# Turning x and the softmax's weights in 32-wide blocks on VectorE instead of on TensorE, from the fourth batch on

## The chip, the cores and the metric

One Trainium2 chip, one core, one launch. The metric is the device time of the whole kernel in microseconds, the median of three runs. Beside it stands one profiled execution, whose trace is what the rows below are read from.

## What is computed

```
q, k, v: (8 batches, 8 heads, 576 positions, 64)           float32
mask: heads 0-3 local (0 <= row - col < 32); heads 4-7 strided (row >= col, row % 32 == col % 32)
attn = softmax(q @ k.T / 8 where mask) @ v
x = attn, heads side by side: (8, 576, 512)
xn = (x - mean) / sqrt(var + 1e-6) * g_ln                  # over the last axis
out = x + relu(xn @ w_ch1) @ w_ch2                         # 512 -> 2048 -> 512
```

## The kernel before, in words

**Two parts in one stream.** The attention of a batch makes x; the feed-forward (FFN) part takes x in chunks of 512 positions, one per batch (positions 0 to 511), and a ninth chunk of the last 64 positions of all batches. Products are exact enough because each operand is held as a high and a low float32r part, and three products are summed (high-high, high-low, low-high).

**Steps.** A run is one chunk; run c does chunk c, in 16 steps f = 0 to 15, one per 128 hidden columns (`steps`, L1005). In a step TensorE does `ffn1` (L758: 12 matmuls into the PSUM tile `ph`, of which there is one), then two halves of `ffn2` (L771: 12 matmuls) with the hidden activations of the step before. From `ph` ScalarE makes `hh` (L749) and VectorE `hl` (L754); `ph` is free for the next `ffn1` when `hl` is made. The runs go in the order 1, 0 (its second half), 2, 3, ... 8; LayerNorm's scale is applied at the end, from x loaded back from DRAM (`residual`, L794, at f = 9 to 14; `close`, L815, in the first step of the next run).

**Visits.** The attention of batches 2 to 7 is woven into the steps. A Pair is two heads of one batch; pairs alternate local and strided, four to a batch, 32 in all. Generator `visits` (L991) makes one visit for each pair i from 7 on, and the main loop takes one piece of it in each step for which `slots[n]` (L1009) is true, between `ffn1` and the first half of `ffn2`. Before, from run 2 on these are the even f, and a visit has two pieces:

- first piece (f = 0, 4, 8, 12): `scores_and_values` (L592). TensorE multiplies the turned weights of pair i (`pt`) by its v, and q by k for pair i+1 (tile `sv`, L637). For pair i+1 VectorE adds the mask (L459) and takes the maximum (L471), GpSimd subtracts it (L475), ScalarE takes the exponential (L480) into `sm`. For pair i VectorE scales the values into `xo` (L649) and SyncE's queue stores `xo` into DRAM (`x_store`, L530; `xdl` for local pairs, `xds` for strided ones, rows in another order). Then v of pair i+2 is loaded (`load_v`, L391), on SyncE's queue.
- second piece, two steps later: `weights_and_x` (L656). TensorE transposes x of pair i (4 tiles of 128x128 for a local pair, 6 for a strided one) and the weights of pair i+1 (6 or 5 tiles) into PSUM (tile `px`, L668). ScalarE makes the high part of x from `px` (L577), VectorE the low part (L582), ScalarE copies the turned weights out (`pt`, L673), and VectorE sums the softmax's rows (L677 to L679, tile `den`).

In the step after a first piece `turn` (L984) turns q and k of pair i+2 on VectorE (`t_half`, L412: L416 local, L418 strided; instruction STREAM_TRANSPOSE, which turns each 32x32 block by itself) from tile `raw`, and then issues the loads of q and k of pair i+3 into the one `raw` buffer (`load_qk`, L328: eight DMAs on SyncE's queue, each 32 partitions by 18 pieces of 32 values, 128 bytes apiece). The loads put the blocks where 32x32 turns make a whole turn of them.

Each engine and each DMA queue takes its instructions in the order of the program (L1098 to L1107). A DMA that waits holds back what stands behind it in its queue. All buffers of the visits (`raw`, `xo`, `pt`, `px`/`sv`) are single.

Of the kernel before, what the change touches and what calls it, by code (L numbers as in the profile page):

```python
# [8 lines left out]
F32 = mybir.dt.float32  # L9
# [37 lines left out]
def kernel(  # L47
# [10 lines left out]
    nc = tc.nc  # L58
# [132 lines left out]

    w1b, w2b = w1.bitcast(U32), w2.bitcast(U32)
# [121 lines left out]
    class Pair:  # L314
# [13 lines left out]
        def load_qk(self):  # L328

            self.raw = raw_tile(f"raw{self.id}").rearrange("p (i s) -> p i s", i=2)  # L330
            for i, src in enumerate((q, k)):
                for h in range(2):
                    for d in range(2):
                        p0 = 64 * h + 32 * d
                        nc.sync.dma_start(  # L335
                            self.raw[p0:p0 + 32, i].rearrange("p (g e) -> p g e", e=32),
                            src[self.b, self.h0 + h].rearrange("(g t) d -> t g d", t=32)[
                                :, :, 32 * d:32 * d + 32])
# [52 lines left out]
        def load_v(self, once=False):  # L391
            dma = nc.sync.dma_start
# [159 lines left out]

        def x_views(self):
# [102 lines left out]
    def weights_and_x(px, p):  # L656
# [14 lines left out]
        if p:  # L671
            p.pt = smp.tile([P, NS, P], F32, tag="pt", name=f"pt{p.id}")
            nc.scalar.copy(out=p.pt[:, 0:p.nt].rearrange("p t x -> p (t x)"),  # L673
                           in_=ps[:, P * n_x:P * (n_x + p.nt)])
            den = stp.tile([P, 2, NS], F32, tag="den", name=f"den{p.id}", bufs=2)
            p.den = den[:, :, 0:p.nt]
            nc.vector.reduce_sum(p.den, p.smv, axis=AX.X)  # L677
            nc.vector.tensor_scalar(p.den, p.den, 1e-9, None, op0=ALU.add)
            nc.vector.reciprocal(out=p.den, in_=p.den)  # L679
# [304 lines left out]
    def turn():  # L984
        while todo:
            i = todo.pop()
            pairs[i].t_piece()
            if 2 * NHP <= i + 1 < NP:
                pairs[i + 1].load_qk()

    def visits():  # L991

        for i in range(2 * NHP - 1, NP):
            p = pairs[i + 1] if i + 1 < NP else None
            pv = pairs[i] if i >= 2 * NHP else None
            scores_and_values(pv, p)
            turned(i + 2)
            if pv and i + 2 < NP:
                pairs[i + 2].load_v()
            yield  # L1000
            weights_and_x(pv, p)
# [6 lines left out]
    for n, (r, f) in enumerate(steps):  # L1008
        slots[n] = (r is runs[1] and f in (11, 13) or r is runs[2]  # L1009
                    or r is not runs[1] and r.c + 1 < B and f % 2 == 0)  # L1010
# [127 lines left out]
```

## Time and profile before

| | |
|---|---|
| median of 3 runs | 928.85 us (927.37 to 929.29) |
| the profiled execution, its own time | 928.84 us |
| span of the profiled execution | 927.1 us |
| TensorE matmul busy | 908.8 us, 98% of the span |
| TensorE weight load busy | 748.5 us, 81% |
| VectorE, ScalarE, GpSimd busy | 409.6, 225.0, 155.4 us (44%, 24%, 17%) |
| granted TensorE clock, mean over the span | 0.995 of full speed |

The span is what the trace covers; 1.7 us of the execution's time lie around it. Matmuls are pipelined, so the busy time of TensorE counts overlaps; what a group of matmuls takes from the whole is read from the chain of work that ended last, where each piece starts at the end of the piece before it.

### The profile page before, as it was taken

What the parts mean: (1) busy time and instruction counts of PE and PEld (TensorE: products, weight loads), DVE (VectorE), ACT (ScalarE), POOL (GpSimd) and SP (SyncE); (2) the same over time, 40 slices, a digit from 0 to 9 for tenths busy, and PEclk for the clock granted to TensorE, in tenths of its full rate; (3) what the DMA queues carried; (4) which work ended last, traced back from release to release, by engine and by line L of the source; (5) the groups of instructions that cost most, each with busy time, mean ns of one, the idle gap of its engine ahead of it and who ended that gap; (6) DMA issues with size and microseconds to landing.
All of it is one profiled execution on the core that took longest, in us unless ns stands there. A gap on an engine that the chain in (4) does not pass through costs nothing.

```text
span 927.1 us, 18224 instructions
## 1 busy us (share of the span) xinstructions
PE 908.8 (98%) x7668; PEld 748.5 (81%) x7668; DVE 409.6 (44%) x784; ACT 225.0 (24%) x378; POOL 155.4 (17%) x191
## 2 busy tenths in 40 slices
PE   6899999999999999999999999999999999999997
PEld 4678888888888888888888888888888888888886
DVE  5887573447743354435433453434443321122123
ACT  4765563112212111211112121112121111111110
POOL 6776385101100010001000110001000000000000
PEclk9999999999999999999999999999999999999999
DMA  9989961247652435243423334243511130002001
GB/s 202 213 181 262 235 201 35 38 100 158 117 105 52 98 64 109 53 76 86 104 40 59 85 64 89 48 98 64 109 28 48 36 108 18 0 1 91 1 1 45
DMA packets 227353, 81.62 MB, mean 88 GB/s; under 512 B 180560, under 2 KB 218184, under 8 KB 227272
## 3 DMA queue, kind: packets, MB, share of 16 engines
q1 hardware_dynamic: 226344, 79.93, 38.4%
q8 instruction: 60, 0.98, 0.4%
q10 hardware_dynamic: 928, 0.53, 0.2%
q14 instruction: 21, 0.17, 0.1%
HBM read 60.25 MB, written 20.18 MB: 87 GB/s over the span
## 4 chain that ended last, share of the span: by engine, by line
PE 93%; DMA 3%; SPq 2%; ACT 0%; DVE 0%; issue 0%; POOL 0%; DVEq 0%; POOLq 0%
PE po L768 42%; PE ph L739 28%; PE ph L743 14%; PE sv L637 5%; PE px L668 3%; DMA rows<-in_k_dram 2%; PE po_last L768 1%; DMA s<-in_moe_w_ch_dram 1%; SPq L335 1%; DMA v_l<-in_v_dram 1%; SPq L346 0%; SPq L406 0%; PE cm L262 0%; SPq L350 0%; PE px L727 0%
## 5 line engine op out<-in xcount | busy, mean ns | idle before, releaser
L768 PE MATMUL po<-w,hh 128*128 128x512 f32 x1120 | 351.3, 395 | 0.8 <-DVE hl L754 0.8
L754 DVE SCALAR_TENSOR_TENSOR hl<-ph,hh 128x512 fp32r<-128x512 f32 x144 | 99.6, 692 | 448.4 <-ACT hh L749 448.4
L768 PEld LDWEIGHTS po<-w,hh 128*128 128x128 f32 x1120 | 205.4, 188 | 42.6 <-ACT pt L490 0.9
L739 PE MATMUL ph<-xh,w 128*128 128x512 f32 x568 | 222.2, 391 | 0.0
L739 PE MATMUL ph<-xl,w 128*128 128x512 f32 x568 | 221.1, 389 | 0.0
L768 PE MATMUL po<-w,hl 128*128 128x512 f32 x560 | 218.1, 390 | 0.0
L749 ACT ACTIVATE hh<-ph 128x512 fp32r<-128x512 f32 x144 | 86.0, 597 | 501.5 <-PE ph L743 501.2
L743 PE MATMUL ph<-xh,w 128*128 128x512 f32 x568 | 152.2, 390 | 0.0
L743 PEld LDWEIGHTS ph<-xh,w 128*128 128x128 f32 x568 | 106.6, 188 | 22.3
L739 PEld LDWEIGHTS ph<-xh,w 128*128 128x128 f32 x568 | 106.7, 188 | 21.9
L739 PEld LDWEIGHTS ph<-xl,w 128*128 128x128 f32 x568 | 106.7, 188 | 21.8
L768 PEld LDWEIGHTS po<-w,hl 128*128 128x128 f32 x560 | 105.1, 188 | 22.4
L475 POOL TENSOR_TENSOR sm<-sm,mx 128x640 f32<-128x640 f32 (+1 forms) x32 | 40.6, 1270 | 358.9 <-DVE mx L471 358.9
L720 POOL TENSOR_TENSOR rs<-rs,mhalf 128x1 f32<-128x1 f32 x36 | 19.7, 549 | 354.5 <-DVE rs L719 354.5
L480 ACT ACTIVATE sm<-sm 128x640 f32<-128x640 f32 (+1 forms) x32 | 23.7, 742 | 106.0 <-POOL sm L475 106.0
L582 DVE TENSOR_TENSOR xl<-px,xh 128x512 fp32r<-128x512 f32 (+2 forms) x48 | 29.9, 661 | 14.4 <-ACT xh L577 14.3
L577 ACT ACTIVATE xh<-px 128x512 fp32r<-128x512 f32 (+2 forms) x48 | 27.5, 646 | 14.7 <-PE px L668 11.2
L231 DVE SCALAR_TENSOR_TENSOR p<-s,p 128x512 uint32<-128x512 uint32 x32 | 22.1, 690 | 11.9 <-ACT p L227 11.8
L471 DVE TENSOR_REDUCE mx<-sm 128x10 f32<-128x640 f32 (+1 forms) x32 | 26.3, 822 | 1.8
L827 DVE SCALAR_TENSOR_TENSOR x<-po,rs,x 128x512 f32<-128x512 f32 (+1 forms) x36 | 24.4, 729 | 1.4 <-PE po L768 1.1
L673 ACT COPY pt<-px 128x640 f32<-128x640 f32 (+1 forms) x24 | 18.0, 748 | 26.9 <-DVE xl L582 26.9
L715 DVE BATCH_NORM_STATS2 st<-x 128x6 f32<-128x512 f32 x36 | 24.0, 667 | 0.0
(126 smaller groups left out, 667.7 us busy)
## 6 DMA issues: line engine op xcount, KB each, us to landing
s<-in_moe_w_ch_dram SPq DMA_DIRECT2D x32, 512.0 KB
out_dram<-x SPq DMA_DIRECT2D x32, 256.0 KB
raw<-in_q_dram SPq DMA_DIRECT2D x104, 72.0 KB
raw<-in_k_dram SPq DMA_DIRECT2D x104, 72.0 KB
v_l<-in_v_dram SPq DMA_DIRECT2D x32, 144.0 KB
xdl<-xo SPq DMA_DIRECT2D x16, 256.0 KB
x<-xdl SPq DMA_DIRECT2D x32, 128.0 KB
x<-xds SPq DMA_DIRECT2D x32, 128.0 KB
```

The lines of the kernel that those rows point to most:

```text
L471: engine(self.mx[:, :, 0:nt], self.smv, axis=AX.X)
L475: nc.gpsimd.tensor_tensor(out=sm, in0=sm, in1=mx[:, :, 0:nt].unsqueeze(3).broadcast_to([P, 2, nt, w]), op=ALU.subtract)
L577: nc.scalar.activation(out=dst(xh), in_=src, func=AF.Copy)
L582: nc.vector.tensor_tensor(out=dst(xl), in0=src, in1=dst(xh).bitcast(F32), op=ALU.subtract)
L637: nc.tensor.matmul(dst, at, by, start=True, stop=True, tile_position=pos)
L668: nc.tensor.transpose(ps[:, P * t:P * (t + 1)], src, ident)
L739: nc.tensor.matmul(ph, w1h[:, cc], x[:, cc, :], start=(n == 0), stop=False)
L743: nc.tensor.matmul(ph, w1l[:, cc], xh[:, cc, :], start=False, stop=(cc == NCC - 1))
L749: nc.scalar.activation(out=hh, in_=ph, func=AF.Relu)
L754: nc.vector.scalar_tensor_tensor(out=hl, in0=ph, scalar=0.0, in1=hh.bitcast(F32), op0=ALU.max, op1=ALU.subtract)
L768: nc.tensor.matmul(po, hx[:, cs], w, start=(start and n == 0), stop=(stop and n == 2))
L827: nc.vector.scalar_tensor_tensor(out=x[:, d], in0=po, scalar=rs, in1=x[:, d], op0=ALU.mult, op1=ALU.add)
```

## The change

From pair 12 on (batch 3; run 2 and later), a visit has three pieces, at f = 0, 2, 3 of every four steps, and TensorE turns nothing in it. Pieces before that are as they were.

- first piece, as before, then `spread`: SyncE's queue stores the weights `sm` of pair i+1 into a DRAM scratch (`wd`), loads x of pair i back from `xdl`/`xds` in four DMAs as 32-wide blocks (tile `sx`, in the buffer of `pt`), and then the weights from `wd` in four DMAs the same way (tile `sp`, in the buffer of `xo`).
- second piece (f + 2): v of pair i+2 is loaded, from ScalarE's queue instead of SyncE's.
- third piece (f + 3), `turn_blocks`: VectorE turns `sx` in place, ScalarE makes x's high part from it, VectorE sums the softmax's rows, makes x's low part, and turns `sp` into `pt`. Then ScalarE's queue issues the k half of `raw` of pair i+3; the q half stays where it was, on SyncE's queue.

```diff
+    wd = [dram.tile([NS * P, P], F32, name=f"wd{i}") for i in range(2)]
...
         def load_qk(self):
...
+            self.load_half(0)
+            self.load_half(1)
+
+        def load_half(self, i, queue=nc.sync):
+            if not i:
+                self.raw = raw_tile(f"raw{self.id}").rearrange("p (i s) -> p i s", i=2)
+            src = (q, k)[i]
+            for h in range(2):
+                for d in range(2):
+                    p0 = 64 * h + 32 * d
+                    queue.dma_start(...
...
-        def load_v(self, once=False):
-            dma = nc.sync.dma_start
+        def load_v(self, once=False, queue=nc.sync):
+            dma = queue.dma_start
...
+        def row_sums(self):
+            den = stp.tile([P, 2, NS], F32, tag="den", name=f"den{self.id}", bufs=2)
+            self.den = den[:, :, 0:self.nt]
+            nc.vector.reduce_sum(self.den, self.smv, axis=AX.X)
+            nc.vector.tensor_scalar(self.den, self.den, 1e-9, None, op0=ALU.add)
+            nc.vector.reciprocal(out=self.den, in_=self.den)
...
+    def spread(px, p):
+
+        if p:
+            d = wd[int(p.local)]
+            nc.sync.dma_start(
+                d.rearrange("(t p) x -> p t x", p=P)[:, 0:p.nt],
+                p.sm[:, 0:p.nt].rearrange("p t h x -> p t (h x)"))
+        if px:
+            cs = P * px.n0
+            t = smp.tile([P, NS, P], F32, tag="pt", name=f"sx{px.id}")
+            px.sx = t.rearrange("p t x -> p (t x)")[:, 0:CH]
+            to_blocks(px.sx, (
+                xd_l[px.b][0:CH, cs:cs + P].rearrange("(j c) d -> c j d", c=STR) if px.local else
+                xd_s[px.b][0:S, cs:cs + P].rearrange("(c j) d -> c j d", j=NB)[:, 0:CH // STR]))
+        if p:
+            t = smp.tile([P, NS, 2, D], F32, tag="xo", name=f"sp{p.id}")
+            p.sp = t.rearrange("p t h d -> p (t h d)")[:, 0:p.nt * P]
+            to_blocks(p.sp, d[0:p.nt * P].rearrange("(j c) x -> c j x", c=32))
+
+    def to_blocks(dst, src):
+        for g in range(4):
+            r = slice(32 * g, 32 * g + 32)
+            nc.sync.dma_start(dst[r].rearrange("p (j e) -> p j e", e=32), src[:, :, r])
+
+    def turn_blocks(px, p):
+
+        if px:
+            nc.vector.transpose(px.sx, px.sx)
+            xh, xl = (t[:, px.h0 // 2, :] for t in x_t(px.b))
+            nc.scalar.activation(out=xh, in_=px.sx, func=AF.Copy)
+        if p:
+            p.row_sums()
+        if px:
+            nc.vector.tensor_tensor(out=xl, in0=px.sx, in1=xh.bitcast(F32), op=ALU.subtract)
+        if p:
+            p.pt = smp.tile([P, NS, P], F32, tag="pt", name=f"pt{p.id}")
+            nc.vector.transpose(
+                p.pt[:, 0:p.nt].rearrange("p t x -> p (t x)"), p.sp)
...
             if 2 * NHP <= i + 1 < NP:
-                pairs[i + 1].load_qk()
+                pairs[i + 1].load_half(0)
+                if i < 3 * NHP + 2:
+                    pairs[i + 1].load_half(1)
...
             scores_and_values(pv, p)
+            by_blocks = i >= 3 * NHP
+            if by_blocks:
+                spread(pv, p)
             turned(i + 2)
+            if by_blocks:
+                yield
             if pv and i + 2 < NP:
-                pairs[i + 2].load_v()
+                pairs[i + 2].load_v(queue=nc.scalar if by_blocks else nc.sync)
             yield
-            weights_and_x(pv, p)
+            (turn_blocks if by_blocks else weights_and_x)(pv, p)
+            if by_blocks and i + 3 < NP:
+                pairs[i + 3].load_half(1, nc.scalar)
             yield
...
         slots[n] = (r is runs[1] and f in (11, 13) or r is runs[2]
-                    or r is not runs[1] and r.c + 1 < B and f % 2 == 0)
+                    or r is not runs[1] and r.c + 1 < B and f % 4 != 1)
```

## Rows read from the trace of the kernel before

**Rows 1.** The page: busy time and share of the span of each engine, and the shares of the chain that ended last by engine.
```profile
PE 908.8 (98%) x7668; PEld 748.5 (81%) x7668; DVE 409.6 (44%) x784; ACT 225.0 (24%) x378; POOL 155.4 (17%) x191
PE 93%; DMA 3%; SPq 2%; ACT 0%; DVE 0%; issue 0%; POOL 0%; DVEq 0%; POOLq 0%
```

**Rows 2.** The chain of work that ended last, from 299 to 324 us (a visit's four steps in run 2, local pair in the first place): start us, us, what, times.
```profile
299.18 0.82 PE sv L637 x55
300.00 0.92 PE sv L637 x47
300.92 2.94 PE po L768 x12
303.86 1.81 PE ph L739 x8
305.67 0.91 PE ph L743 x4
306.58 2.72 PE po L768 x12
...
312.03 1.09 PE px L668 x10
313.12 2.75 PE po L768 x12
...
318.59 2.72 PE po L768 x12
321.31 1.81 PE ph L739 x8
```

**Rows 3.** The same chain at other visits: a strided pair in the first place, and the last visit (pair 31, nothing but x left).
```profile
336.89 1.20 PE px L668 x11
338.09 2.75 PE po L768 x12
...
734.61 0.65 PE px L668 x6
```

**Rows 4.** The instructions of L668 from 249 us, where run 2 begins, to 745 us: duration ns min/median/max, first and last start.
```profile
L668 PE MATMUL px<-ident,sm x105: 272/273/273, 262.5 to 711.5; 128*128 128x128 f32 x105
L668 PE MATMUL px<-ident,xo x100: 272/273/273, 262.0 to 735.0; 128*128 128x128 f32 x100
```

**Rows 5.** The timeline from 299 to 316 us, the engines beside TensorE and SyncE's queue (SPq, where the time is that of the issue): start us, us, what, idle time before it and what ended that.
```profile
302.70 0.93 DVE L649 TENSOR_TENSOR xo<-sv,den 128x256 f32<-128x256 f32 x3
...
303.96 0.50 SPq L536 DMA_DIRECT2D xdl<-xo  x1
304.26 0.75 ACT L480 ACTIVATE sm<-sm 128x648 f32<-128x648 f32 x1 [4.39 <-POOL sm L475]
...
307.92 0.77 DVE L416 STREAM_TRANSPOSE qt_l<-raw 128x576 f32<-128x576 f32 x1
308.61 0.74 DVE L416 STREAM_TRANSPOSE kt_l<-raw 128x576 f32<-128x576 f32 x1
...
313.16 0.60 ACT L577 ACTIVATE xh<-px 128x512 fp32r<-128x512 f32 x1 [0.43 <-PE px L668]
313.79 0.69 DVE L582 TENSOR_TENSOR xl<-px,xh 128x512 fp32r<-128x512 f32 x1 [0.34 <-ACT xh L577]
...
314.40 0.82 DVE L677 TENSOR_REDUCE den<-sm 128x12 f32<-128x648 f32 x1
...
315.25 0.17 DVE L678 TENSOR_SCALAR den<-den 128x12 f32<-128x12 f32 x1
315.46 0.23 DVE L679 RECIPROCAL den<-den 128x12 f32<-128x12 f32 x1
```

**Rows 6.** The timeline around the end of a step's `ffn1` (318.59 us in rows 2), ScalarE and VectorE.
```profile
318.69 0.60 ACT L749 ACTIVATE hh<-ph 128x512 fp32r<-128x512 f32 x1 [3.37 <-PE ph L743]
319.32 0.69 DVE L754 SCALAR_TENSOR_TENSOR hl<-ph,hh 128x512 fp32r<-128x512 f32 x1 [3.63 <-ACT hh L749]
319.93 0.69 DVE L715 BATCH_NORM_STATS2 st<-x 128x6 f32<-128x512 f32 x1
```

**Rows 7.** The store of `xo` in the DMA engines, in halves of a microsecond: us, busy time of each engine, granted clock, share of the 16 DMA engines, GB/s.
```profile
304.00:304.50 0.50, 0.50 (x4) 0.42 (x3) 0.00 (x0) 0.24 (x1) 0.23 (x1) 1.00 0.13 39
304.50:305.00 0.50, 0.50 (x4) 0.42 (x3) 0.00 (x0) 0.50 (x1) 0.00 (x0) 1.00 0.92 293
```

**Rows 8.** A load of `raw` with nothing beside it: the timeline of SyncE's queue, the time being that of the issue.
```profile
285.31 1.93 SPq L335 DMA_DIRECT2D raw<-in_q_dram  x4
287.29 2.12 SPq L335 DMA_DIRECT2D raw<-in_k_dram  x4
```

**Rows 9.** The DMA engines at the end of that load, in the columns of rows 7.
```profile
290.00:290.50 0.50, 0.50 (x4) 0.42 (x3) 0.50 (x2) 0.00 (x0) 0.00 (x0) 1.00 0.92 146
290.50:291.00 0.50, 0.50 (x4) 0.42 (x3) 0.50 (x3) 0.31 (x1) 0.00 (x0) 1.00 0.21 25
```

**Rows 10.** The DMA queue from 285.0 to 291.5 us, that load and little else: packets, MB, share of the time of the 16 engines.
```profile
q1 hardware_dynamic: 4736, 0.59, 56.7%
```

**Rows 11.** DMA issues over the whole span by line: duration of the issue ns min/median/max, first and last start.
```profile
L335 SPq DMA_DIRECT2D raw<-in_q_dram x104: 311/495/2133, 44.1 to 659.7; - x104
...
L836 ACTq DMA_DIRECT2D out_dram<-x x5: 530/567/709, 920.7 to 923.5; - x5
```

**Rows 12.** VectorE's block transposes over the whole span, local ones with a dense output and strided ones with a scattered one: ns min/median/max, first and last start.
```profile
L416 DVE STREAM_TRANSPOSE qt_l<-raw x13: 767/769/770, 52.6 to 656.7; 128x576 f32<-128x576 f32 x13
...
L418 DVE STREAM_TRANSPOSE qt_s<-raw x13: 1247/1248/1256, 69.9 to 681.6; 128x576 f32<-128x576 f32 x13
```

**Rows 13.** The DMA queue from 249 to 745 us, in the columns of rows 10.
```profile
q1 hardware_dynamic: 135953, 34.97, 34.3%
```

More of the change, by code (lines that the diff above doesn't have):

```diff
@@ L328, in load_qk @@
         def load_qk(self):
[L330 to L338, printed above, removed]
+            self.load_half(0)
[7 more added lines that the diff above has]
+                    p0 = 64 * h + 32 * d
+                    queue.dma_start(
+                        self.raw[p0:p0 + 32, i].rearrange("p (g e) -> p g e", e=32),
+                        src[self.b, self.h0 + h].rearrange("(g t) d -> t g d", t=32)[
+                            :, :, 32 * d:32 * d + 32])
         def load_rows(self):
@@ L674, in weights_and_x @@
                            in_=ps[:, P * n_x:P * (n_x + p.nt)])
[L675 to L679, printed above, removed]
+            p.row_sums()
[26 more added lines that the diff above has]
+        if p:
+            p.row_sums()
+        if px:
[4 more added lines that the diff above has]
+                p.pt[:, 0:p.nt].rearrange("p t x -> p (t x)"), p.sp)
     def split_x(hi, lo, src):
```

## The prediction

> **What bounds the kernel now.** I read the shares of the page first: TensorE holds 93% of the chain that ended last, VectorE is busy 44% of the span and ScalarE 24% [rows 1]. So an instruction taken from TensorE is worth its time on the chain, as long as nothing makes TensorE wait in its place. Next the chain in order of time, over the four steps of one visit [rows 2]: its pieces are TensorE's alone and follow each other without a gap. A step without a piece of a visit is one `ffn2` and one `ffn1`, 2.72 + 2.72 = 5.44 us (306.58 to 312.03). The transposes of the second piece are a piece of their own there, 1.09 us, and the `ffn2` behind them takes 2.75 us instead of 2.72. That is how the busy time of a transpose (273 ns, [rows 4]) is to be read: ten of them overlap and take 1.09 us from the whole, not 2.73.
>
> **What is removed from TensorE.** Run 2 begins at 249 us, and from there 105 transposes of weights and 100 of x are in the trace [rows 4]. They belong to visits 12 to 31: ten visits with a local pair in the first place (4 + 6 tiles), nine with a strided one (6 + 5) and the last (6), 100 + 99 + 6 = 205, so all of them go. Their price on the chain is 1.09 us for ten [rows 2], 1.20 for eleven and 0.65 for six [rows 3], each with 0.03 for the slower `ffn2` behind: 10 x 1.12 + 9 x 1.23 + 0.68 = **22.95 us**. Scores and values stay as they are.
>
> **What is added, and whether it is in time.** I take the visit whose first piece starts at 299.18 [rows 2].
>
> *The way through DRAM.* `xo` is whole at 303.63, its last store is issued by 304.46, and the exponential ends at 305.01 [rows 5]. What a store takes to land no row shows, because nothing waits for it soon. From below: the store fills the DMA engines within a microsecond of its issue [rows 7]. The nearest complete case is the load of `raw`: issue ended 289.41 [rows 8], last packets in 290.5 to 291.0 [rows 9], about 1.5 us later. I take 1.5 us, and twice that, 3.0, as the upper end, since a receipt may follow the last packet. SyncE's queue then runs: store of the weights issued 305.05 to 305.55, landed 307.05; x landed at 305.96, four loads at the 0.50 us that the like loads of `raw` take (495 ns, [rows 11]), to 307.96; four loads of the weights, whose 24 pieces per partition against 18 I price at 0.66 us each, to 310.6; landed at **312.1**. With 3.0 us for each landing it is 315.1. The engines allow it: the eight loads are 2048 + 3072 pieces of 128 bytes, and the load of `raw` shows 0.567 x 16 x 6.5 us / 4736 = 12.5 ns for such a piece [rows 10], so 4.0 us on 16 engines, less than the 4.6 us of issuing.
>
> When are they wanted? Call E the end of `ffn1` in the step of the third piece. It is 318.59 before [rows 2] and 317.47 without the transposes. VectorE comes to the blocks behind `hl`, at E + 1.34 (318.59 to 319.93, [rows 6]), which is 318.8. So the blocks are there 6.7 us early, 3.7 at the upper end. The wait costs nothing; SyncE's queue, held for some 5 us more, has behind it only the q half of `raw`, wanted a step after the next first piece, LayerNorm's reloads of x and output stores, wanted no sooner than a step later.
>
> *VectorE in the third piece.* Turning x: 0.77 us for 576 columns with a dense output, so 0.68 for 512 [rows 12]. Row sums 1.29 us (314.40 to 315.69, [rows 5]); the high part of x, 0.60 us on ScalarE, lies beside them. The low part 0.69. Turning the weights 0.85 us (640 columns) or 1.03 (768). Sum 3.69 us for the longer, so from E + 1.34 to E + 5.03. Values and scores of the next visit want the weights after one `ffn2` and one `ffn1`, at E + 5.44. That leaves **0.4 us**: the narrowest cover of the change. Upper end: both turns at the price of the scattered ones, 1.25 us for 576 [rows 12], that is 1.11 and 1.39 or 1.67; then the weights are late by 0.38 us in nine visits and 0.66 in ten. I take the dense price, since both outputs are dense. x is wanted by the next run only behind a batch's last visit, its low part by the eighth matmul, E + 2.72 + 7 x 0.23 = E + 4.3, against E + 4.0; late by 0.1 us at the upper end, five times.
>
> *ScalarE.* It loses the copy of `pt`, which cost the chain nothing, and issues DMAs. Four or six for v stand between `hh` of one step (ending E + 0.70, by [rows 6]) and that of the next, 4.8 us later. Its own issues, few and at the end, took 0.57 us, at most 0.71 [rows 11], so six are 3.4 to 4.3 us: covered. Four for the k half of `raw` stand behind the high part of x, from about E + 2.7 to E + 5.0, and the next `hh` is due at E + 5.5: covered, and a late `hh` has room there, because `ph` is wanted again only at E + 5.44 + 1.74 + 2.94 = E + 10.1 (scores and values, and the `ffn2` behind them, [rows 2]).
>
> *The DMA engines altogether.* 94,720 pieces of 128 bytes are added to 135,953 packets in 496 us at 34.3% [rows 13]; at 12.5 ns each they are 74 us on 16 engines, about 15 points more, and the stores of the weights a few: some 55%. Nothing else in the stretch waits closely for a transfer.
>
> **A rule that speaks against it.** The blocks move as the load of `raw` moves, at 12.5 ns a piece [rows 10]. The Trainium skill, page "VectorE: DVE Perf Modes", section "The three transpose paths", warns that a plain DMA copy which does a transpose by its strides is 19 times slower than the crossbar transpose when the innermost destination stride is large. By that rule the loads would outlast a visit, and the kernel would be slower by far more than it gains. Here the innermost runs are 32 dense values and VectorE turns inside them, so by the row I let the rule have no part in the sum; as a mechanism it is the second rival.
>
> **The sum.** The profiled execution took 928.84 us, span 927.1, and agrees with the median of 928.85. 928.84 - 22.95 = **905.9 us**, with nothing given back.
>
> **Rivals.**
> - *VectorE's third piece is too long.* TensorE then stands before values and scores. For it: only 0.4 us of cover. Against: dense outputs, and neighbouring VectorE instructions overlap by some 0.08 us (307.92 + 0.77 against 308.61, [rows 5]). At the upper end 9 x 0.38 + 10 x 0.66 = 10 us come back: 915.9. It can lie anywhere from there down to the forecast. Chance 0.15.
> - *The blocks land late, slower than before.* VectorE waits in order, and TensorE with it. If each of the eight loads took the longest issue seen, 2.13 us [rows 11], the weights would land at 305.96 + 17.0 + 1.5 = 324.5 and be turned at 325.5, where 322.9 was wanted: 19 x 2.6 = 49 us, so 955. It decides against the change from 22.95 / 19 = 1.2 us per visit on, that is from a landing 11 us later than worked out. For it: two trips through DRAM in a row. Against: 6.7 us to spare, and engines half idle. Chance 0.05.
> - *ScalarE's issues hold back `hh`.* `hh` and `hl` take 1.4 us [rows 6], so `hh` must start by E + 8.7, and the four issues may take 1.5 us each before TensorE waits; the six for v, in a plain step whose `ph` is wanted at 5.44 + 2.72, about 1.0 each. At 1.8 us for the k half, 17 visits lose about 1.2 us: 926. For it: issues of 2.13 us occur on SyncE's queue when the DMA engines are full [rows 11]. Against: they are half empty here. Chance 0.04.
>
> **How the numbers follow.** The forecast has 0.76. A measurement of this kernel can tell 0.2%, 1.9 us, from no change. The forecast's own range is 904.0 to 907.8; the range of 904.0 to 911.5 takes in the lower half of the first rival and leaves out its upper half and the other two, about 0.18. Faster by over 0.2%: the forecast, the first rival and half of the third, 0.93. Within 0.2%: 0.02, from the third. Slower: 0.05.
>
> **What would show it.** Right: 47 transposes left at L668, all before 249 us; steps of 5.44 us at the third piece; the chain without a gap; VectorE with no wait for a DMA at its turns, the issues of the weights' loads ending some 11.5 us after a first piece's start. The first rival would show as idle time of TensorE before `sv`, ended by VectorE's turn of `pt`; the second as VectorE waiting for a DMA at a turn; the third as `hh` starting late behind ScalarE's issues. Wrong I would be if any of these came to 0.3 us or more in most visits.

## The result and the profile after

The changed kernel takes 912.46 us (median of 4 runs, 910.85 to 914.09), the kernel before 928.93 us beside it (927.37 to 929.29): ratio 0.9826, 95% interval 0.9801 to 0.9851. It is faster by 16.5 us. The forecast was 905.9 with a range of 904.0 to 911.5, so the direction is right and the time lies 0.96 us above the range. The profiled execution took 913.76 us with a span of 910.8.

The page, and TensorE's transposes of line 682 (line 668 before, [rows 4]): count, duration ns min/median/max, first and last start.

```profile
span 910.8 us, 18090 instructions
PE 888.8 (98%) x7463; PEld 727.4 (80%) x7463; DVE 431.4 (47%) x813; ACT 206.0 (23%) x349; POOL 155.6 (17%) x191
```
```profile
L682 PE MATMUL px<-ident,sm x27: 272/273/273, 177.8 to 245.2; 128*128 128x128 f32 x27
L682 PE MATMUL px<-ident,xo x20: 272/273/273, 202.1 to 244.9; 128*128 128x128 f32 x20
```

47 transposes are left, all before run 2, as forecast. The chain over one visit answers to [rows 2] (start us, us, what):

```profile
298.40 1.74 PE sv L651 x102
300.14 2.94 PE po L817 x12
...
311.25 2.72 PE po L817 x12
313.97 1.81 PE ph L788 x8
315.78 0.91 PE ph L792 x4
316.69 2.72 PE po L817 x12
...
322.12 1.74 PE sv L651 x102
```

The `ffn2` of 316.69 follows `ffn1` without a gap, and takes 2.72 us. From one visit's first piece to the next are 23.72 us (23.73 with a strided pair in the first place): four steps of 5.44, 1.74 for scores and values and 0.22 more for the slower `ffn2` behind them. Before, it was 24.85 us with a local pair in the first place and 24.97 with a strided one (299.18 to 324.03 to 349.00 on the chain of before). The differences, 1.13 and 1.24 us, are those of the forecast (1.12 and 1.23) within 0.01.

Four visits do not look like this: the last of runs 2, 3, 4 and 5 (steps 12 to 15). Behind them the next first piece comes after 25.20, 25.29, 25.04 and 24.53 us, **5.2 us** too late in all. The last visit of run 6 has no v to load, and TensorE does not wait in it. The waits of TensorE that the profile shows from 249 to 745 us are these seven (us in total, times, longest); in the trace of before it shows none:

```profile
PE ph L788 <- DVE xl L724: 1.7, 4, 0.4
PE ph L788 <- DVE hl L803: 1.3, 3, 0.5
```

The view counts 3.0 us of idle time; the rest of the 5.2 goes where matmuls that would overlap start afresh. The chain at the end of run 2's last visit:

```profile
334.07 0.92 PE ph L792 x4
...
335.07 0.61 ACT hh L798
...
335.70 0.53 DVE hl L803
336.24 4.56 DMA raw<-in_q_dram
340.80 0.02 issue
340.82 2.65 DMA v_s<-in_v_dram
343.47 0.69 DVE sx L718
...
345.91 0.50 PE ph L788
346.41 0.93 PE ph L792 x4
347.33 1.74 PE sv L651 x102
```

This is read from the end: TensorE waits for VectorE's work on x, before that stands a DMA of v on ScalarE's queue, and that one began 0.02 us after a DMA of the **q half of `raw`**, issued by SyncE at 336.24, had landed. One link is to be read with care: the turn of x (`sx`) does not need the DMA of v. The four loads of its own blocks had landed by 334.64, by their semaphore events. VectorE comes to it straight from `hl`, and `hl` waited for `hh` on ScalarE:

```profile
342.85 0.69 DVE L803 SCALAR_TENSOR_TENSOR hl<-ph,hh 128x512 fp32r<-128x512 f32 x1 [1.51 <-ACT hh L798]
343.45 0.70 DVE L718 STREAM_TRANSPOSE sx<-sx 128x512 f32<-128x512 f32 x1
```

The issues themselves, ScalarE and its queue (ACTq; the time of a group runs from its first issue to the end of its last):

```profile
335.07 0.60 ACT L798 ACTIVATE hh<-ph 128x512 fp32r<-128x512 f32 x1 [4.84 <-PE ph L792]
335.35 6.49 ACTq L413 DMA_DIRECT2D v_s<-in_v_dram  x6
342.21 0.60 ACT L798 ACTIVATE hh<-ph 128x512 fp32r<-128x512 f32 x1 [6.55 <-DMA v_s<-in_v_dram]
```

`ffn1` ends at 340.43 (334.99 + 5.44), so `hh` was due at 340.53 and started at 342.21, because it stands behind v's six issues. TensorE pays for that twice: it stands idle for 0.46 us before the next `ffn1`, behind `hl`, and for 0.43 us before the eighth matmul of that `ffn1`, behind x's low part (`xl`), since VectorE's third piece has moved back with `hl`. In run 5's last visit only the second of the two waits occurs, and the visit is 0.81 us too long. The same group in other visits: the first two are ordinary visits, the third is run 3's last, and the fourth the last pair of all, with no q half and no reload beside it.

```profile
288.14 3.85 ACTq L413 DMA_DIRECT2D v_s<-in_v_dram  x6
...
384.25 4.21 ACTq L413 DMA_DIRECT2D v_s<-in_v_dram  x6
432.81 5.80 ACTq L413 DMA_DIRECT2D v_s<-in_v_dram  x6
...
672.48 2.33 ACTq L413 DMA_DIRECT2D v_s<-in_v_dram  x6
```

One issue of the 54 by itself is short (ns min/median/max), so most of a group's time lies between its issues:

```profile
L413 ACTq DMA_DIRECT2D v_s<-in_v_dram x54: 279/283/512, 288.1 to 674.4; - x54
```

**What lies between them.** In the built program each DMA of SyncE's and ScalarE's queues signals one of eight semaphores (counters that a landing DMA raises and that an engine or a queue can wait for). They are handed out in turn, over both queues together, without an exception among the 798 DMAs. Before it is issued, a DMA waits until the one that had its semaphore last has landed, that is the DMA eight places before it in the program. The six of run 2's last visit, in the program's list of waits:

```
L413 DMA v_s<-in_v_dram 18x11x64 [waits DMAHW7]
L413 DMA v_s<-in_v_dram 18x11x64 [waits DMAHW1]
L413 DMA v_s<-in_v_dram 18x10x64 [waits DMAHW3]
L413 DMA v_s<-in_v_dram 18x11x64 [waits DMAHW4]
L413 DMA v_s<-in_v_dram 18x11x64 [waits DMAHW5]
L413 DMA v_s<-in_v_dram 18x10x64 [waits DMAHW6]
```

The trace's semaphore events say when each of those landed:

| issue of v, us | the DMA it waits for (SyncE's) | issued | landed |
|---|---|---|---|
| 335.35 | weights, first piece | 332.94 | 335.33 |
| 336.60 | weights, third piece | 333.96 | 336.58 |
| 337.75 | reload of x, local half | 335.06 | 337.73 |
| 340.17 | reload of x, strided half | 335.61 | 340.15 |
| 340.82 | q half, first piece | 336.24 | 340.80 |
| 341.56 | q half, second piece | 336.70 | 341.54 |

Each issue comes 0.02 us after the landing. In all four last visits the gap is at most 0.07 us, and one of the six waits for the strided half of the reload, which lands 4.5 to 4.9 us after its issue. In an ordinary visit the six wait for the weights' loads (2.4 to 2.7 us from issue to landing) and two of the q half (3.2 to 3.7). For the group at 672.48 everything had landed at least 1.26 us before; its issues follow each other every 0.4 us.

The third piece on VectorE (start us, us, what), for an `ffn1` that ends at E = 316.69:

```profile
317.35 0.69 DVE L803 SCALAR_TENSOR_TENSOR hl<-ph,hh 128x512 fp32r<-128x512 f32 x1 [4.69 <-ACT hh L798]
317.96 0.70 DVE L718 STREAM_TRANSPOSE sx<-sx 128x512 f32<-128x512 f32 x1
318.59 0.78 DVE L563 TENSOR_REDUCE den<-sm 128x12 f32<-128x648 f32 x1
...
319.76 0.63 DVE L724 TENSOR_TENSOR xl<-sx,xh 128x512 fp32r<-128x512 f32 x1
320.42 0.98 DVE L727 STREAM_TRANSPOSE pt<-sp 128x768 f32<-128x768 f32 x1
```

And SyncE's queue ahead of it, and the DMA queues from 249 to 745 us (packets, MB, share of 16 engines), which answer to [rows 13]:

```profile
304.23 0.39 SPq L695 DMA_DIRECT2D wd<-sm  x1
305.12 2.10 SPq L713 DMA_DIRECT2D sx<-xdl  x4
307.33 2.13 SPq L713 DMA_DIRECT2D sp<-wd  x4
```
```profile
q1 hardware_dynamic: 178306, 43.23, 42.2%
q10 hardware_dynamic: 71846, 12.84, 17.3%
```

### The profile page after: what moved, and what is told of

It reads as the page before. It is cut to its first block, busy times and chain, and to the rows that moved or that the text cites. A ratio compares the mean times of both kernels' runs of the same rounds, so it can differ in the third digit from the quotient of the medians.

```text
span 910.8 us, 18090 instructions
## 1 busy us (share of the span) xinstructions
PE 888.8 (98%) x7463; PEld 727.4 (80%) x7463; DVE 431.4 (47%) x813; ACT 206.0 (23%) x349; POOL 155.6 (17%) x191
## 4 chain that ended last, share of the span: by engine, by line
PE 87%; DMA 7%; SPq 2%; DVE 2%; ACT 1%; issue 1%; POOL 0%; ACTq 0%; DVEq 0%; POOLq 0%
PE po L817 39%; PE ph L788 26%; PE ph L792 13%; PE sv L651 5%; DMA raw<-in_q_dram 2%; PE po_last L817 1%; DMA rows<-in_k_dram 1%; DMA s<-in_moe_w_ch_dram 1%; DMA v_l<-in_v_dram 1%; SPq L342 1%; DMA rows<-in_q_dram 1%; PE px L682 1%; DMA x<-xds 1%; ACT hh L798 1%; DMA v_s<-in_v_dram 0%
## 5 line engine op out<-in xcount | busy, mean ns | idle before, releaser
L487 ACT ACTIVATE sm<-sm 128x640 f32<-128x640 f32 (+1 forms) x32 | 23.8, 744 | 104.7 <-POOL sm L482 104.7
L764 DVE BATCH_NORM_STATS2 st<-x 128x6 f32<-128x512 f32 x36 | 24.1, 668 | 15.8 <-DMA x<-xds 15.8
L663 DVE TENSOR_TENSOR xo<-sv,den 128x256 f32<-128x256 f32 (+1 forms) x72 | 24.0, 389 | 0.0
L239 DVE SCALAR_TENSOR_TENSOR r<-s,p 128x512 uint32<-128x512 uint32 x32 | 21.9, 685 | 1.6
L223 ACT ACTIVATE s<-s 128x512 f32<-128x512 f32 x32 | 21.4, 671 | 5.1 <-DMA s<-in_moe_w_ch_dram 5.1
```

What stands on the lines that cost most here:

```text
L487: nc.scalar.activation(out=self.smv, in_=self.smv, func=AF.Exp, scale=SCALE)
L663: nc.vector.tensor_tensor(out=xot[0:n, :, t0:t1], in0=src, in1=pv.den[0:n, :, t0:t1].unsqueeze(3).broadcast_to([n, 2, t1 - t0, D]), op=ALU ...
L764: nc.vector.bn_stats(st, x)
```

## The experiments

All start from the changed kernel. "Distance" is the time from the first piece of a last visit (runs 2, 3, 4, 5) to the next first piece; all others are 23.7 to 23.9 unless told (e7 has another of 27.12, e12 one of 24.83, e15 two of 24.7 and 24.8; for e2 and e14 see below). Where the kernel before stands beside, the ratio to it is given with its interval.

| run | us | ratio to before | distances |
|---|---|---|---|
| changed kernel | 912.46 | 0.9826 [0.9801, 0.9851] | 25.20 25.29 25.04 24.53 |
| e1_v_sync | 906.26 | 0.9750 [0.9722, 0.9778] | 23.76 23.75 23.75 23.79 |
| e2_reload_early | 911.30 | 0.9801 [0.9773, 0.9830] | 23.75 23.75 23.82 23.84 |
| e3_turn_earlier | 907.04 | 0.9760 [0.9734, 0.9785] | 23.75 23.76 23.75 23.76 |
| e4_long_turn | 922.30 | 0.9919 [0.9895, 0.9942] | 26.0 to 26.4, ordinary 24.0 to 24.2, one 24.47 |
| e5_all_sync | 906.51 | 0.9757 [0.9732, 0.9783] | 23.74 23.78 24.31 23.73 |
| e6_sync_turn_earlier | 943.46 | 1.0151 [1.0107, 1.0195] | up to 29.55 |
| e7_q_later | 916.27 | 0.9862 [0.9838, 0.9886] | 24.70 25.25 24.95 24.59 |
| e8_v_split | 910.24 | 0.9801 [0.9774, 0.9827] | 23.87 23.86 26.60 24.17 |
| e9_q_scalar | 916.53 | 0.9863 [0.9843, 0.9883] | 25.93 27.81 26.80 25.41 |
| e10_changed_again | 911.92 | 0.9821 [0.9804, 0.9838] | 25.30 25.39 24.87 24.52 |
| e11_v_sync_again | 907.35 | 0.9774 [0.9757, 0.9792] | 23.73 23.75 23.83 23.73 |
| e12_q_scalar_reload_early | 912.65 | 0.9825 [0.9797, 0.9853] | 25.64 24.61 25.08 25.10 |
| e13_v_sync_reload_early | 908.00 | 0.9764 [0.9744, 0.9784] | 23.75 23.76 23.75 23.75 |
| e14_reload_gpsimd | 909.38 | 0.9778 [0.9761, 0.9796] | 23.82 23.82 23.85 23.82 |
| e15_q_in_eight | 913.48 | 0.9827 [0.9812, 0.9843] | 24.68 26.21 24.55 24.83 |

**v on SyncE's queue (e1, and again beside the unchanged kernel, e10 and e11).**

```diff
-                pairs[i + 2].load_v(queue=nc.scalar if by_blocks else nc.sync)
+                pairs[i + 2].load_v()
```

> The changed kernel with one part undone: v of the next pair is issued from SyncE's queue again, at the same place. In the changed kernel the four first pieces 25.2, 25.3, 25.0 and 24.5 us after those before them (all others 23.72) make 5.2 us, each at the end of a run. Theory 1 (ScalarE's six issues for v, 5.8 to 6.8 us there, hold back the next step's first activation): it starts on time, the four distances fall to 23.7 to 23.9, the span to about 904.5 after an opening like that of the kernel before. Theory 2 (LayerNorm's last reload, queued behind the block loads, arrives when VectorE is wanted): VectorE still waits some 4 us for it, the distances stay above 24.5, the time as the changed kernel's. Theory 3 (the third piece is too tight for the next run's x even when on time): distances of 24.0 to 24.3.

> The changed kernel unaltered, beside the two others on one chip: 912.5, between 910.8 and 914.1, four distances of 24.5 to 25.3 us.

> The version with v on SyncE's queue once more, for its distance to the changed kernel on one chip: 906.3, all distances 23.75, so 5 to 6 us below the changed kernel.

All four stalls go, and the time is the 905.9 us of the forecast within 0.4 (e1) to 1.5 us (e11). On one chip the edit is worth 911.92 - 907.35 = 4.6 us, against 5.1 us of excess distance in e10's trace. VectorE still waits for LayerNorm's last reload, as long as in the changed kernel (3.64 us idle, against 3.85), and that costs nothing: ScalarE and VectorE at the end of run 2's last visit in e1.

```profile
338.99 0.60 ACT L798 ACTIVATE hh<-ph 128x512 fp32r<-128x512 f32 x1 [4.78 <-PE ph L792]
```
```profile
338.56 0.69 DVE L764 BATCH_NORM_STATS2 st<-x 128x6 f32<-128x512 f32 x1 [3.64 <-DMA x<-xds]
...
339.62 0.69 DVE L803 SCALAR_TENSOR_TENSOR hl<-ph,hh 128x512 fp32r<-128x512 f32 x1
```

`hh` starts on time and ends at 339.59, and `hl` follows 0.03 us later, when LayerNorm's operations on VectorE are just through: the reload is the next thing that would bind here. In e1 the profile shows no wait of TensorE from 249 to 745 us.

**The k half too (e5).**

```diff
-                pairs[i + 2].load_v(queue=nc.scalar if by_blocks else nc.sync)
+                pairs[i + 2].load_v()
...
-                pairs[i + 3].load_half(1, nc.scalar)
+                pairs[i + 3].load_half(1)
```

> As the run with v on SyncE's queue, and the k half of raw too (issued in the third piece, on SyncE's queue): ScalarE issues nothing in the visits. Theory 1 (only the six issues for v, in a step whose activation has 1.2 us of room, cost something; the four of the k half stand before an activation with 3 us of room): the same time as with v alone, 906.3 +- 0.7, first pieces 23.75 us apart. Rival (the k half's issues cost something too): 1 us or more less. Rival (SyncE's queue has no room left): LayerNorm's reloads or the block loads come later, long distances at the ends of runs.

906.51 us, the same as e1 within the spread of the runs (904.36 to 908.34): the k half in the third piece costs nothing that shows on ScalarE's queue. What its issues wait for had landed 0.5 to 6 us before in the two visits of the changed kernel from 298 to 347 us. One visit of 24.31 is left in e5's trace, with TensorE waiting for x's low part.

**The reloads a step earlier (e2, and with v on SyncE's queue e13).**

```diff
-            if 0 <= i < NT:
-                x = x_load(self.c, i)
+            j = i + int(1 < self.c < B - 1)
+            if 0 <= j < NT:
+                x = x_load(self.c, j)
```

> The changed kernel with LayerNorm's four reloads of x issued one step earlier (f = 8 to 11 in runs 2 to 6), so that none stands behind the block loads of f = 12. Theory 1 (ScalarE's issues of v): the wait of VectorE for x vanishes, the issues of v still take 5 us or more because the other transfers are still there, the four long distances stay at 24.4 to 25.3, the time changes by less than 1.5 us from the changed kernel. Theory 2 (the reload): the distances fall to 23.7, about 5 us less.

> v on SyncE's queue and the reloads a step earlier. With v on SyncE's queue VectorE's wait for the last reload (3.6 us) ended just in time, since the distances were 23.75 there: so no gain, 905.6 to 907.4. If the reload still costs something hidden, 1 us or more less.

In e2 the last visits are whole, and two others stall instead (25.96 and 24.23), a visit earlier, where v's four issues now stand beside the reloads (ScalarE and its queue):

```profile
504.13 0.32 ACTq L405 DMA_DIRECT2D v_l<-in_v_dram  x1
507.38 0.32 ACTq L406 DMA_DIRECT2D v_l<-in_v_dram  x1
508.42 0.32 ACTq L405 DMA_DIRECT2D v_l<-in_v_dram  x1
510.47 0.32 ACTq L406 DMA_DIRECT2D v_l<-in_v_dram  x1
510.89 0.60 ACT L798 ACTIVATE hh<-ph 128x512 fp32r<-128x512 f32 x1 [7.55 <-DMA v_l<-in_v_dram]
```

By the semaphore events they waited for a reload landed at 504.11, two pieces of the q half (507.36, 508.40) and a reload (510.45). The stall moves with the reloads, so neither forecast came: the four distances fell, and the time did not fall by 5 us. e13 shows no stall and gains nothing over e1, so a late reload by itself cost nothing there.

**The turn a step earlier (e3), and both (e6).** The turn of the blocks and the k half go to the step before v's:

```diff
+                turn_blocks(pv, p)
+                if i + 3 < NP:
+                    pairs[i + 3].load_half(1, nc.scalar)
+                yield
                 pairs[i + 2].load_v(queue=nc.scalar if by_blocks else nc.sync)
-            yield
-            (turn_blocks if by_blocks else weights_and_x)(pv, p)
-            if by_blocks and i + 3 < NP:
-                pairs[i + 3].load_half(1, nc.scalar)
-            yield
+            if not by_blocks:
+                weights_and_x(pv, p)
+                yield
```

e6 has `load_v()`, on SyncE's queue, in that place.

> The changed kernel with the two later pieces exchanged: VectorE turns the blocks at f + 2 and ScalarE issues the k half there, v is issued by ScalarE at f + 3. Theory 1: v's issues now stand before an activation that has 3 us of room, so the long distances go, unless the four issues of the k half take their place; time about 5 us less than the changed kernel's. Theory 3: the long distances go too, since x is ready a step earlier. Theory 2: the wait for the reload stays and with it stalls of up to 1 us. What can spoil it: at f + 2 the weights' blocks land 0 to 1.5 us after VectorE wants them (the last issue ends about 0.8 us before, in strided visits 0.2 us after, and a landing takes some 1.5 us), seen as VectorE waiting for a DMA at a turn; TensorE does not stand for it while the third piece ends before the next activation's turn, 2 us later.

> Both of the earlier ways together: v on SyncE's queue, and the turn of the blocks a step earlier (f + 2, v at f + 3). Theory 1: each removed the same loss, so together they are worth no more than either, 906.0 to 907.0. Theory 3 (a second loss, from the third piece, remains in the run with v on SyncE's queue): below 905.5.

e3 came out as expected, e6 37 us slower than expected and slower than the kernel before. The same k half in the same visit, first e3, then e6:

```profile
264.79 2.28 ACTq L342 DMA_DIRECT2D raw<-in_k_dram  x4
```
```profile
264.24 4.73 ACTq L342 DMA_DIRECT2D raw<-in_k_dram  x4
269.07 0.60 ACT L798 ACTIVATE hh<-ph 128x512 fp32r<-128x512 f32 x1 [4.36 <-DMA raw<-in_k_dram]
```

In e3 all that it waits for had landed 1 us before. In e6 v's DMAs on SyncE's queue come in between in the program, the turn of the semaphores shifts, and the k half waits for two pieces of the q half, landed 266.67 and 268.63, issued 0.02 us later. `hl` then held TensorE 11 times, up to 3.9 us. So in these two runs it is not the engine that makes a group of issues long but what stands eight places before it.

**The cover on VectorE (e4).** The turn of the weights is done twice:

```diff
             nc.vector.transpose(
                 p.pt[:, 0:p.nt].rearrange("p t x -> p (t x)"), p.sp)
+            nc.vector.transpose(
+                p.pt[:, 0:p.nt].rearrange("p t x -> p (t x)"), p.sp)
```

> The changed kernel with the turn of the weights done twice, one after the other with the same result: 0.8 to 0.9 us more of VectorE in each third piece. In the changed kernel the turned weights are ready 0.7 us (768 columns) or 0.9 us (640) before TensorE wants them. If that cover is as read, TensorE waits 0.1 to 0.3 us before the scores and values behind ten of the visits and hardly behind the others: the time is 1 to 4 us above the changed kernel's. If the cover is wider than read (the activation that VectorE waits for is the true limit), the time does not change.

9.8 us over the changed kernel, more than expected. 0.98 us more on VectorE cost an ordinary visit 0.45 to 0.49 (768 columns), 0.84 more 0.27 (640), and the four last visits lost 0.9 to 1.5 us more than in the changed kernel. The first turn ends at 320.86 and the second at 321.87, TensorE's `ffn1` ahead at 321.59 (chain of e4):

```profile
321.59 0.38 issue
321.97 1.91 PE sv L651 x102
```

So the cover is about 0.98 - 0.47 = 0.5 us, near the forecast's 0.4; from E + 4.71 alone it would be 5.44 - 4.71 = 0.73, and that is why less was expected here.

**Where the other loads stand (e7, e8, e9, e12).** e7 calls the q half in the third piece; e9 also issues it on ScalarE's queue; e12 is e9 with e2's reloads; e8 splits v by head, the second head in the third piece.

```diff
-                pairs[i + 1].load_half(0)
                 if i < 3 * NHP + 2:
+                    pairs[i + 1].load_half(0)
                     pairs[i + 1].load_half(1)
...
+                pairs[i + 3].load_half(0)
                 pairs[i + 3].load_half(1, nc.scalar)
```
```diff
-                pairs[i + 2].load_v(queue=nc.scalar if by_blocks else nc.sync)
+                pairs[i + 2].load_v(
+                    queue=nc.scalar if by_blocks else nc.sync, heads=(0,) if by_blocks else (0, 1))
...
+            if by_blocks and i + 2 < NP:
+                pairs[i + 2].load_v(queue=nc.scalar, heads=(1,))
```

> The changed kernel with v still issued by ScalarE at f + 2, but the q half of raw moved from the step before to the third piece (SyncE's queue, just ahead of ScalarE's k half), so that SyncE issues little beside v. If v's six issues are slow because SyncE's queue loads at the same time: in the last visits of the runs they fall from 5.8 to 6.8 us to 4 or less and the long distances go (time 906 to 907.5; LayerNorm's last reload still stands beside them). If six issues on ScalarE's queue are slow by themselves in that step: they stay near 6 us and so does the time, 911 to 913.

> The changed kernel with v's issues, all on ScalarE's queue as there, split by head: the first half at f + 2, the other in the third piece behind the high part of x and ahead of the k half. Theory 1: three issues at f + 2 take 3.5 us at most and end before the next activation is due, so the long distances go; the seven issues of the third piece take 3.5 to 5 us and end before the activation behind them runs out of its 3 us of room: 906 to 908. If the transfers as such are the cause and not the place of the issues in ScalarE's order: no change, 911 to 913.

> Moving the q half within SyncE's queue changed nothing because that queue runs ahead of the steps: the q half was still issued right behind the block loads, at the time of v. Here the q half too is issued by ScalarE, in the third piece behind the high part of x, together with the k half (eight issues), and v's six stay on ScalarE at f + 2: SyncE's queue then has nothing for the visit behind the block loads, except LayerNorm's reload in a run's last visit. If v's issues are stretched by what SyncE's queue moves at the same time: six take about 2.4 us in ordinary strided visits (3.9 to 4.2 in the changed kernel) and 4 or less in the last ones (5.8 to 6.8), and the long distances go: 906 to 908. If six issues on ScalarE's queue take long by themselves: 4 and 6 us as before, 911 to 913. What can spoil it: eight issues in the third piece, 4 to 5 us, may reach past the room of the next activation, then every distance grows.

> All of raw on ScalarE's queue in the third piece, v on ScalarE's queue at f + 2, and LayerNorm's reloads a step earlier (f = 8 to 11). If the reload is what held the last visits in the version without this last edit: VectorE's wait of 4 to 7 us for it goes, v's six issues take 2.3 to 3 us in all strided visits, the four distances of 25.4 to 27.8 fall to about 23.8, and the time from 916.5 to 907 +- 1. If it is the eight issues of raw on ScalarE (next activation late): they stay above 25.

e7 did not test what it was for: SyncE's queue runs ahead of the steps, and the q half was issued at 289.40 all the same, right behind the weights. Its last visits are much as in the changed kernel, and 3.4 of the 3.8 us that it takes more lie in the visit of 27.12, where three of v's four issues waited for pieces of the reload and of the q half that landed 5.2 to 6.9 us after their issue. In e9 v's six came down to 4.2 to 4.3 us in the last visits, near the 4 expected, and the last visits grew longer, by the reload (VectorE of e9, `hl` due at 339.9):

```profile
341.38 0.69 DVE L764 BATCH_NORM_STATS2 st<-x 128x6 f32<-128x512 f32 x1 [6.14 <-DMA x<-xds]
...
342.39 0.68 DVE L803 SCALAR_TENSOR_TENSOR hl<-ph,hh 128x512 fp32r<-128x512 f32 x1
```

e8 stalled in one visit for the same reason (VectorE idle for 6.45 us before that operation). e12 took the reload away from there, and eight issues of `raw` on ScalarE then waited for the reloads, one of them until 319.64 for a strided half issued at 310.30; two more issues took 1.4 and 1.7 us by themselves. ScalarE stood idle for 7.7 us before `hh`. The expected 907 was missed for that.

**A wait or contention (e14, e15).** Both keep every byte. e14 issues the reloads from GpSimd's queue, whose DMAs have other semaphores; e15 loads the q half by eight DMAs in place of four, which shifts the turn.

```diff
-                x = x_load(self.c, i)
+                x = x_load(self.c, i, queue=nc.gpsimd)
```
```diff
-                    queue.dma_start(a, c)
+                    n = 9 if self.b >= 3 and not i else 18
+                    for g in range(0, 18, n):
+                        queue.dma_start(a[:, g:g + n], c[:, g:g + n])
```

> LayerNorm's reloads of x are issued by GpSimd's queue in place of SyncE's; the bytes and the step stay. Theory of the semaphores: the program has eight semaphores for the DMAs of SyncE's and ScalarE's queues, taken in turn, and each DMA waits at its issue until the DMA eight before it in the program has landed. In the last visits of runs 2 to 5 one of v's six waits so for the strided half of the reload (issued 335.61, landed 340.15 in the changed kernel, v's fourth issued at 340.17). With the reload on GpSimd's queue, which has semaphores of its own, v's six wait for the weights' four loads and two of the q half, as in the ordinary visits: about 4 us in the last visits too in place of 6.3, distances 23.7 in place of 24.5 to 25.3, 906 to 907.5 us. Theory of contention (an issue takes longer while the DMA engines or the issuing hardware are busy with the reload and the q half): the same transfers run at the same time, so still about 6 us, distances 24.5 to 25.3, 911 to 912.5 us.

> The q half of raw is loaded by eight DMAs of half the size in place of four, from run 2 on; bytes, queue and step stay, SyncE issues four more a visit. Theory of the semaphores: the turn of the eight is shifted. By the built program's waits, v's six no longer wait for the reload's strided half in the last visits of runs 2, 4 and 5 (SyncE's fifth or a later piece of the q half does), and still do in run 3, there by the second of the six. So the six take about 4 to 5 us in runs 2, 4 and 5, with distances of 23.7 to 24.2, and about 6 us in run 3 with 25 or more; two of the six then wait for v's own first two. About 908 us, 906.5 to 910. Theory of contention: the same bytes and more issues beside them, so the six take 6.3 us or more in all four last visits and about 4 or more in the others; distances of 24.5 to 25.5 in all four, 911 to 914 us.

In e14 v's six in the last visits take 3.35, 4.30, 4.26 and 3.89 us, and their distances are 23.8: the wait theory's prediction. The time came to 909.4, not 907, because new stalls stand a visit earlier (25.22, 24.15, 25.17, 24.19). There v's third issue waits for a piece of the weights (ScalarE's queue in e14):

```profile
311.38 0.32 ACTq L406 DMA_DIRECT2D v_l<-in_v_dram  x1
315.42 0.32 ACTq L405 DMA_DIRECT2D v_l<-in_v_dram  x1
```

That piece was issued at 308.36 and landed at 315.40, with the strided reload issued on GpSimd's queue at 307.90. In e15 v's six took 6.2 to 6.4 us in all four, where 4 to 5 had been expected in three. The waits were the ones read from the program (run 2's no longer met the strided half), but the q half's first piece, issued at 333.87, landed only at 337.88, 4.0 us later. And run 3, where the second of the six waits for the strided half until 435.10, is the longest (26.21), as expected. The time, 913.48, is where the other theory had put it (911 to 914). So two things multiply: **the issue is a wait for a landing**, and **landings come late beside the strided reload**. The first is shown issue by issue; no run changed how the strided half is moved (what the traces say of it stands at the end).

## Why the prediction was right and wrong

- **22.95 us for 205 transposes: right.** e1, the change without its one flaw, takes 906.26 us where 905.9 was forecast, and its visits are 23.74 and 23.75 us apart where they were 24.85 and 24.97. That the time agrees to 0.4 us is in part luck: e5, e11 and e13, also without the flaw, take 906.5 to 908.0.
- **The way through DRAM: right.** The weights' loads were issued by 309.46, 11.1 us after the first piece; the forecast had 11.4. VectorE's waits have none for them, so the second rival did not come. From its issue a store of x lands after 2.0 to 2.4 us (local) or 2.8 to 3.9 (strided), one of the weights after 2.9 to 5.1; behind the issue's end 1.5 had been taken, and 3.0 as the upper end. The load of the weights takes 2.2 to 3.7. The last piece landed at 311.94, 6.0 us before VectorE came to the turns (317.96); the forecast had 6.7.
- **VectorE's third piece: right**, E + 4.71 against E + 5.03. The turns cost 0.70, 0.84 and 0.98 us (dense price 0.68, 0.85, 1.03), and the cover is as narrow as forecast: e4. TensorE never waited before `sv`, so the first rival did not come.
- **The DMA engines: near as a mean** (42.2 + 17.3 = 59.5% against some 55%), wrong as an argument. "They are half empty here" is a mean over 496 us; the landing that counts stands in the five us of a reload, where the share is 0.55 to 1.08 in the halves of a microsecond from 335.5 to 340.5.
- **ScalarE's issues of v: wrong.** The step was "Its own issues, few and at the end, took 0.57 us, at most 0.71 [rows 11], so six are 3.4 to 4.3 us: covered". An issue costs less than that, 0.28 to 0.51 us. What was left out is that a moved DMA takes its wait along: on SyncE's queue [rows 8, 11] it holds only other DMAs, on ScalarE's it holds `hh`. The six took 3.8 to 4.2 us in ordinary visits, at the edge of the 4.8 us between two `hh`, and 5.8 to 6.8 in the last. That is the 5.2 us. The third rival named the place where this shows (`hh` late behind ScalarE's issues), and rightly; it had a chance of 0.04, and its price was put on the k half, where the wait cost nothing (e5). Its threshold, about 1.0 us each for v, was near (0.97 to 1.13), but it looked at `ph` alone. The shorter cover in a last visit is that of x's low part, forecast as E + 4.0 against E + 4.3 with `hl` on time: a late `hh` used it up in all four, in run 5 without any wait for `hl`.
- **LayerNorm's reloads "wanted no sooner than a step later": wrong, without cost as a wait of VectorE's.** The last one is waited for, 15.8 us in four visits, and ends just in time; where anything delays it, it binds (e8, e9). Its strided half took 4.1 to 5.9 us to land in the trace of before already, by its semaphore events.
- **The rest.** The span of 927.1 less 22.95 plus 5.2 is 909.4, against 910.8. What is left lies in the opening, whose code is the same: run 2's first full visit starts at 250.89 instead of 249.28, and anywhere from 247.21 to 252.25 in the runs above.

The Trainium skill, page "DMA: Bandwidth & Descriptors", section "Issuing engines are not separate DMA queues", says that issuing on several engines saves only the sequencer's time for the issue, and that this is usually small beside the DMA itself. The trace agrees: one of v's issues takes 0.28 us and lands 2.0 to 5.3 us after its start, six with nothing to wait for take 2.33 us, and taking them from SyncE gained nothing (e1, e5).

## What to carry to other kernels

A DMA that is moved to a compute engine's queue brings its semaphore wait along: before moving it, look in the built program for the DMA it waits for, and at when that one lands in the trace, since everything behind it on the engine waits as well. Price the landing from the stretch where it happens, not from a mean share or a quiet row. The best versions here keep v on SyncE's queue, whose waiting holds no arithmetic (906.3 to 908.0 us in e1, e5, e11 and e13), or let it stand where everything before it has landed (e3, 907.0).

## What was not expected of the hardware

The reload's strided half (128 runs of 1 KB) lands 4.1 to 8.4 us after its issue in the changed kernel, 6.2 in the median, its local half 4.1 in the median, a weights' load of 80 to 96 KB in 128-byte pieces 2.6. Beside the strided half weights' loads took up to 7.2 us (e14) and a piece of the q half 4.2 to 6.2 (the last visits of the changed kernel). Some issues took long by themselves in such stretches, 1.4 to 2.0 us on ScalarE's queue (e12) and up to 3.0 on SyncE's (e14); what held them no row tells.

The trace of the changed kernel narrows the cause down. In run 2's last visit 256 packets of 1 KB move, 128 for each half. The first 128, by the order of the issues those of the local half, run from 336.43 to 337.15 us, up to 21 at a time. The other 128 run from 337.40 to 339.45, for the most part four and never more than six at a time. The local half raises its semaphore in 16 events (2.17 to 2.67 us after its issue), the strided half in 5 (one at 0.94, four from 4.46 to 4.53). And it seems to hold others in part: in e1 the q half's first piece beside it (issued at 334.56) has twelve of its 16 events by 2.14 us and the last four from 3.53 to 4.13. This looks as if the strided half ran on four of the 16 DMA engines and other loads' shares on those four stood behind it. That is not shown: the packets do not say which engine moved them, and no run spread the strided half wider.
